# Moving the low-order subtraction of the first token block from GpSimd to VectorE

## The chip, the cores and the metric

The kernel runs on one core of one Trainium2 chip. The metric is device time in microseconds (us). Engines are named as the profile names them: PE (TensorE matmul) and PEld (its weight load), DVE (VectorE), ACT (ScalarE), POOL (GpSimd) and SP (SyncE, which here only issues DMAs).

## The reference

Three layers follow one another: windowed attention, a gated feed-forward layer on all tokens, and a layer of 8 experts of which each token uses one. The change lies in the second:

```python
def _moe_ref(x, w_gate, w_val, w_out, rms_g):        # x: 2304 x 512, d_ff = 1536
    rms = np.sqrt(np.mean(x * x, axis=-1, keepdims=True) + 1e-06)
    xn = x / rms * rms_g
    g = xn @ w_gate
    silu = g * (1.0 / (1.0 + np.exp(-g)))
    val = xn @ w_val
    return (silu * val @ w_out).astype(np.float32)
```

## The kernel before

**Split products.** Every matrix product is made of three matmuls. An operand is split into a high part, which is the operand rounded to the type fp32r, and a low part, which is the operand less its high part; the product is high x high + high x low + low x high (`split_mm`). So each operand costs one cast, always on ACT, and one subtraction, on DVE or POOL.

**Tokens, blocks, units.** The 2304 tokens are six parts of 384 (`subs`), gathered into four blocks (`BLOCKS`): the first two blocks hold two parts each, the last two hold one. The hidden width of 1536 is cut into 12 slices of 128. A *unit* is one slice for one part, so the first block has 24 units. For unit u the kernel does the following.

- `gate_val(u)`: 24 matmuls on PE write the gate product to one PSUM bank and the value product to another. In the first block these are nearly always the same two banks.
- `silu(u)`: ACT takes tanh of the gate bank into the tile `t` (L592), DVE makes silu times value in two steps (L593 reads the gate bank, L594 the value bank), ACT casts `t` to the high part `hh` (L595), and a subtraction writes the low part `hl` (L596). There is one tile `t`, and there are two each of `hh` and `hl`.
- `out_b(u - 1)`: 9 matmuls on PE with `hh` and `hl` of the unit before.

PE's order is `gate_val(u)`, `out_b(u - 1)`, `gate_val(u + 1)`. The last of these needs the two banks of unit u back, so it waits for L593 and L594 of unit u.

**Other work in the first block.** The weights of this layer come as 64-bit floating-point numbers and are converted on DVE while the first block runs: four instructions for each half slice, L400, L405, L408 and L415 (`w_conv`), with a square on ACT between (L425). The weights are then split (`w_split`): casts on ACT (L549), subtractions on DVE for gate and value (`wla`, L551) and on POOL for the output weights (`wlo`, L551). Also in between lie the normalisations of later parts: L333, L343, L345, L353, L355, L362 and L367 on DVE, L328, L351 and L364 on ACT, and one matmul with a matrix of ones on PE. The order on every engine is written out by the program (`manual_schedule`): after `silu(u)` a loop takes pieces of this other work up to a budget. The wait for an earlier result is taken in that order; an engine does not pass a waiting instruction.

From the second block on, L596 already runs on DVE.

Of the kernel before, what the change touches and what calls it, by code (L numbers as in the profile page):

```python
# [8 lines left out]
F32 = mybir.dt.float32  # L9
# [4 lines left out]
ALU = mybir.AluOpType  # L14
# [35 lines left out]
def attention_moe_moe_kernel(ctx, tc, qT, kT, vw, w1p, rms_g, wg2, wg2T, w2p, out):  # L50
    nc = tc.nc
# [243 lines left out]
    blocks, subs = [], []  # L295
# [275 lines left out]
    def gv_banks(u):  # L571
        n = subs[units[u][1]][2]
        if u == 1 and LEAD > 1:

            return bank[6:8]
        if u % 2 and len(blocks[n][2]) == 1:
            return bank[2:4] if n == len(blocks) - 1 else bank[6:8]
        return bank[0:2]
# [6 lines left out]
    def silu(u):  # L585
        k, i = units[u]
        nt = subs[i][1]
        g, v = (b[:, :nt] for b in gv_banks(u))
        t = t_p.tile([P, SUB], F32, name="t")[:, :nt]
        hh = hh_t["b", u] = h_p.tile([P, 512], F32R, name="hh")  # L590
        hl = hl_t["b", u] = h_p.tile([P, 512], F32R, name="hl")
        nc.scalar.activation(t, g, AF.Tanh, scale=0.5)  # L592
        nc.vector.scalar_tensor_tensor(out=t, in0=t, scalar=1.0, in1=g, op0=ALU.add, op1=ALU.mult)  # L593
        nc.vector.scalar_tensor_tensor(out=t, in0=t, scalar=0.5, in1=v, op0=ALU.mult, op1=ALU.mult)  # L594
        nc.scalar.copy(hh[:, :nt], t)  # L595
        (nc.gpsimd if subs[i][2] == 0 else nc.vector).tensor_tensor(  # L596
            out=hl[:, :nt], in0=t, in1=hh[:, :nt].bitcast(F32), op=ALU.subtract)

    def last_mm(w, h, banks, f0, f1):

# [231 lines left out]
    for u, (k, i) in enumerate(units):  # L832
# [4 lines left out]
        if u == 0:  # L837
            beside([norm1, conv], 3.0)
        silu(u)
        budget = BUDGET[n] + min(spare, 0.5)  # L840

# [213 lines left out]
    with tc.If(n_over > 0):  # L1055
        with tc.For_i(0, n_over, 1) as i:
            ex = nc.values_load(slot[0:1, bass.ds(i, 1)], engines=(ET.SP,), min_val=0, max_val=E - 1)
            row = nc.values_load(slot[0:1, bass.ds(i + NS, 1)], engines=(ET.SP,), min_val=0, max_val=E * NT - 2 * P)
            with tc.tile_pool(name="ovr", bufs=1) as o_p:
# [7 lines left out]
                for j in range(2):  # L1067
                    nc.gpsimd.indirect_dma_start(
                        out=xg[:, j], out_offset=None, in_=x2dram[:, :],
# [9 lines left out]
                for j in range(2):  # L1079
                    for f in range(NF2):  # L1080
# [4 lines left out]
                        out=out[:, :], out_offset=bass.IndirectOffsetOnAxis(ap=ix[:, j, 0:1], axis=0),  # L1085
# [48 lines left out]
```

## Time and profile before

| what | value |
|---|---|
| median of 3 runs | 909.71 us (909.12 to 910.42) |
| the profiled execution | 913.41 us |
| its span, first to last instruction | 911.5 us |
| PE busy over the span | 851.7 us (93%) |
| DVE busy | 671.6 us (74%) |
| ACT busy | 415.7 us (46%) |
| POOL busy | 252.7 us (28%) |

The profiled execution is one run of its own, 3.70 us above the median. Shares over the whole span mix stages: the first block, where L596 is on POOL, starts its first `silu` at 137.7 us, and its last L596 starts at 299.0 us.

### The profile page before, as it was taken

What the parts mean: (1) busy time and instruction counts of PE and PEld (TensorE: products, weight loads), DVE (VectorE), ACT (ScalarE), POOL (GpSimd) and SP (SyncE); (2) the same over time, 40 slices, a digit from 0 to 9 for tenths busy, and PEclk for the clock granted to TensorE, in tenths of its full rate; (3) what the DMA queues carried; (4) which work ended last, traced back from release to release, by engine and by line L of the source; (5) the groups of instructions that cost most, each with busy time, mean ns of one, the idle gap of its engine ahead of it and who ended that gap; (6) DMA issues with size and microseconds to landing.
All of it is one profiled execution on the core that took longest, in us unless ns stands there. A gap on an engine that the chain in (4) does not pass through costs nothing.

```text
span 911.5 us, 13574 instructions
## 1 busy us (share of the span) xinstructions
PE 851.7 (93%) x4667; PEld 778.3 (85%) x4667; DVE 671.6 (74%) x1535; ACT 415.7 (46%) x951; POOL 252.7 (28%) x268
## 2 busy tenths in 40 slices
PE   7999979998999999999999899999899999889994
PEld 7999968887889899999998789888678899778883
DVE  7789979999897677786589975986584665675462
ACT  5777864343343434322343333334463554564352
POOL 3357662332233000000312243232310330333021
PEclk9999998999999999999999999999899999999998
DMA  7888433333422620000100005323574664672010
GB/s 210 287 277 279 152 127 118 105 109 104 139 70 93 156 37 17 1 1 0 36 36 1 1 1 214 126 90 82 167 230 128 210 214 128 213 227 70 3 44 17
DMA packets 40895, 102.96 MB, mean 113 GB/s; under 512 B 10575, under 2 KB 15055, under 8 KB 40658
## 3 DMA queue, kind: packets, MB, share of 16 engines
q1 hardware_dynamic: 35090, 88.29, 30.8%
q0 software_dynamic: 5696, 13.14, 4.6%
q8 instruction: 78, 1.28, 0.6%
q14 instruction: 31, 0.25, 0.1%
HBM read 87.08 MB, written 19.57 MB: 117 GB/s over the span
## 4 chain that ended last, share of the span: by engine, by line
PE 48%; DVE 28%; issue 9%; DMA 6%; POOL 4%; ACT 3%; SPq 0%; DVEq 0%; POOLq 0%; ACTq 0%
PE bank L56 46%; DVE junk L658 6%; DMA out_dram<-x,ix 3%; DVE wla L551 3%; DVE wraw L405 2%; DVE wraw L408 2%; DVE t L594 2%; DVE wraw L415 2%; DVE t L593 2%; DVE wraw L400 2%; DMA sq<-x2dram,ix 1%; PE bank L222 1%; PE bank L785 1%; DVE xt L367 1%; ACT hh L595 1%
## 5 line engine op out<-in xcount | busy, mean ns | idle before, releaser
L56 PE MATMUL bank<-xt,wha 128*128 128x384 f32 (+3 forms) x1728 | 425.2, 331 | 23.0 <-DVE t L593 9.0
L56 PEld LDWEIGHTS bank<-xt,wha 128*128 128x128 f32 x1728 | 307.6, 191 | 42.2 <-DVE t L593 13.4
L56 PE MATMUL bank<-xt,wla 128*128 128x384 f32 (+3 forms) x864 | 284.7, 330 | 8.9 <-DVE wla L551 6.5
L56 PEld LDWEIGHTS bank<-xt,wla 128*128 128x128 f32 x864 | 165.1, 191 | 13.5 <-DVE wla L551 10.1
L56 PE MATMUL bank<-wlo,hh 128*128 128x512 f32 x384 | 152.8, 398 | 0.5 <-POOL wlo L551 0.5
L56 PE MATMUL bank<-who,hl 128*128 128x512 f32 x384 | 152.6, 397 | 0.4 <-DVE hl L944 0.4
L56 PE MATMUL bank<-who,hh 128*128 128x512 f32 x384 | 151.9, 395 | 0.1
L595 ACT CAST hh<-t 128x384 fp32r<-128x384 f32 x72 | 37.0, 513 | 206.4 <-DVE t L594 206.4
L944 DVE SCALAR_TENSOR_TENSOR hl<-bank,hh 128x512 fp32r<-128x512 f32 (+1 forms) x72 | 45.3, 629 | 86.7 <-ACT hh L943 86.6
L551 DVE TENSOR_TENSOR wla<-wraw,wha 128x512 fp32r<-128x512 f32 (+1 forms) x112 | 98.3, 877 | 5.1 <-ACT wha L549 4.6
L658 DVE SCALAR_TENSOR_TENSOR junk<-x,wg_bc 128x512 f32<-128x512 f32 x120 | 91.3, 812 | 0.0
L56 PEld LDWEIGHTS bank<-who,hl 128*128 128x128 f32 x384 | 72.8, 190 | 17.4 <-DVE hl L944 1.2
L549 ACT CAST wha<-wraw 128x512 fp32r<-128x512 f32 (+1 forms) x113 | 87.1, 771 | 0.0
L943 ACT ACTIVATE hh<-bank 128x512 fp32r<-128x512 f32 (+1 forms) x72 | 39.6, 550 | 104.0 <-PE bank L56 104.0
L56 PEld LDWEIGHTS bank<-wlo,hh 128*128 128x128 f32 x384 | 73.0, 190 | 11.9 <-POOL wlo L551 0.8
L56 PEld LDWEIGHTS bank<-who,hh 128*128 128x128 f32 x384 | 73.2, 191 | 11.4 <-issue 0.5
L56 PE MATMUL bank<-kt,qz 128*128 128x128 f32 x288 | 76.2, 406 | 5.5 <-DMA kt<-in_kT_dram 4.7
L551 POOL TENSOR_TENSOR wlo<-wraw,who 128x512 fp32r<-128x512 f32 x30 | 49.0, 1635 | 114.7 <-ACT who L549 114.6
L56 PEld LDWEIGHTS bank<-kt,qz 128*128 128x128 f32 x288 | 72.3, 334 | 6.1 <-DVE qz L165 4.7
L549 ACT CAST who<-wraw 128x512 fp32r<-128x512 f32 x111 | 68.8, 620 | 17.3 <-PE bank L56 17.0
L208 ACT ACTIVATE wraw<-sm,nm 128x128 f32<-128x128 f32 x144 | 56.2, 391 | 26.1 <-DVE nm L204 25.5
L551 DVE TENSOR_TENSOR wlo<-wraw,who 128x512 fp32r<-128x512 f32 x81 | 57.1, 705 | 8.6 <-ACT who L549 3.6
(153 smaller groups left out, 1009.5 us busy)
## 6 DMA issues: line engine op xcount, KB each, us to landing
wraw<-in_w2p_dram SPq DMA_DIRECT2D x64, 512.0 KB, 4.5
st<-in_w1p_dram SPq DMA_DIRECT2D x24, 768.0 KB, 4.4
wraw<-in_vw_dram SPq DMA_DIRECT2D x16, 512.0 KB, 5.1
qz<-in_qT_dram SPq DMA_DIRECT2D x32, 144.0 KB, 5.4
xdram<-wraw SPq DMA_DIRECT2D x16, 288.0 KB, 2.8
x2dram<-x SPq DMA_DIRECT2D x18, 256.0 KB, 2.4
kt<-in_kT_dram SPq DMA_DIRECT2D x15, 288.0 KB, 5.6
xr<-xdram SPq DMA_DIRECT2D x4, 768.0 KB, 5.5
```

Of the source, the lines that this page charges most:

```text
L56: nc.tensor.matmul(o, l, r, start=start, stop=stop)
L208: nc.scalar.activation(p[:, j], sm[:, j], AF.Exp, bias=nm[:, j:j + 1], scale=-1.0, accum_out=rs[:, j:j + 1])
L400: nc.vector.tensor_scalar(out=w, in0=hi, scalar1=3, scalar2=0x3FFFFFFF, op0=ALU.logical_shift_left, op1=ALU.bitwise_and)
L405: nc.vector.scalar_tensor_tensor(out=w, in0=lo, scalar=29, in1=w, op0=ALU.logical_shift_right, op1=ALU.bitwise_or)
L408: nc.vector.scalar_tensor_tensor(out=w, in0=hi, scalar=-0x40000000, in1=w, op0=ALU.bitwise_and, op1=ALU.bitwise_or)
L415: nc.vector.scalar_tensor_tensor(out=wf, in0=gt, scalar=TINY64 * TINY64, in1=wf, op0=ALU.is_ge, op1=ALU.mult)
L549: nc.scalar.copy(wh, src[:, r])
L551: e.tensor_tensor(out=wl, in0=src[:, r], in1=wh.bitcast(F32), op=ALU.subtract)))
L595: nc.scalar.copy(hh[:, :nt], t)
L658: nc.vector.scalar_tensor_tensor(out=junk, in0=x2, scalar=1.0, in1=wg_bc[:, e], op0=ALU.mult, op1=ALU.mult, accum_out=lg[:, j, e:e + 1])
L943: nc.scalar.activation(hh[:, :n], bank[k % 2][:, :n], AF.Relu, scale=1.0)
L944: nc.vector.scalar_tensor_tensor(out=hl[:, :n], in0=bank[k % 2][:, :n], scalar=0.0, in1=hh[:, :n].bitcast(F32), op0=ALU.max, op1=ALU.subtract)
```

## The change

For parts of the first block, L596 is issued on DVE instead of POOL. The place in the program is the same; the operands are the same.

```diff
         nc.vector.scalar_tensor_tensor(out=t, in0=t, scalar=1.0, in1=g, op0=ALU.add, op1=ALU.mult)
         nc.vector.scalar_tensor_tensor(out=t, in0=t, scalar=0.5, in1=v, op0=ALU.mult, op1=ALU.mult)
         nc.scalar.copy(hh[:, :nt], t)
-        (nc.gpsimd if subs[i][2] == 0 else nc.vector).tensor_tensor(
-            out=hl[:, :nt], in0=t, in1=hh[:, :nt].bitcast(F32), op=ALU.subtract)
+        nc.vector.tensor_tensor(out=hl[:, :nt], in0=t, in1=hh[:, :nt].bitcast(F32), op=ALU.subtract)
```

On DVE the 24 subtractions come in directly behind L594 of their units. Two neighbouring units in the middle of the first block show the two patterns; `wraw_109` is a converted weight slice, `st` the raw 64-bit words. The first of the two has a conversion's first step behind it:

```order
 L593 SCALAR_TENSOR_TENSOR t<-t,bank_65 128x384
 L594 SCALAR_TENSOR_TENSOR t<-t,bank_66 128x384
+L596 TENSOR_TENSOR hl<-t,hh 128x384
 L400 TENSOR_SCALAR wraw_109<-st 128x768
 L405 SCALAR_TENSOR_TENSOR wraw_109<-st,wraw_109 128x768
```

L400 now stands behind a subtraction that needs `hh` of the same unit from ACT. The next unit has a conversion's last step behind it:

```order
 L593 SCALAR_TENSOR_TENSOR t<-t,bank_65 128x384
 L594 SCALAR_TENSOR_TENSOR t<-t,bank_66 128x384
+L596 TENSOR_TENSOR hl<-t,hh 128x384
 L415 SCALAR_TENSOR_TENSOR wraw_109<-gt,wraw_109 128x768
 L400 TENSOR_SCALAR wraw_109<-st 128x768
```

Here L415 and the L400 of the next half slice have moved behind the subtraction. On POOL, before, the same part of the program reads (`wlo` and `who` are low and high parts of output weights):

```order
L596 TENSOR_TENSOR hl<-t,hh 128x384 x2
L551 TENSOR_TENSOR wlo_1556<-wraw_108,who_1555 128x512
L596 TENSOR_TENSOR hl<-t,hh 128x384 x2
L551 TENSOR_TENSOR wlo_1560<-wraw_108,who_1559 128x512
L596 TENSOR_TENSOR hl<-t,hh 128x384 x2
L551 TENSOR_TENSOR wlo_1558<-wraw_109,who_1557 128x512
```

and in the changed kernel:

```order
L551 TENSOR_TENSOR wlo_1558<-wraw_107,who_1557 128x512
L551 TENSOR_TENSOR wlo_1556<-wraw_108,who_1555 128x512
L551 TENSOR_TENSOR wlo_1560<-wraw_108,who_1559 128x512
L551 TENSOR_TENSOR wlo_1558<-wraw_109,who_1557 128x512
L551 TENSOR_TENSOR wlo_1556<-wraw_109,who_1555 128x512
```

Only the weight subtractions are left there in this stage. The orders of PE, ACT and SP hold the same instructions as before in the same sequence.

## Rows read from the trace of the kernel before

**Rows 1.** Chain of waits, 139 to 279 us, its shares by engine and line.
```profile
by line: DVE wraw L405 15.9%; DVE wraw L408 14.7%; DVE wraw L415 12.7%; DVE wraw L400 10.9%; PE bank L56 10.1%; DVE t L594 6.4%; DVE t L593 5.8%; DVE wla L551 4.9%; DVE xt L367 3.9%; issue 3.2%; DVE sq L333 2.2%; ACT sq L328 1.3%; DVE sq L3
```

**Rows 2.** Stages: us, PE, PEld, DVE, ACT, POOL busy (instructions), PE clock, DMA, GB/s.
```profile
139.00:279.00 140.00, 131.28 (x655) 118.91 (x653) 132.02 (x156) 55.98 (x95) 42.70 (x30) 0.97 0.32 103
224.00:231.00 7.00, 7.00 (x31) 6.73 (x30) 6.23 (x9) 2.63 (x5) 1.66 (x2) 0.76 0.39 134
279.00:305.00 26.00, 25.38 (x134) 23.72 (x134) 15.12 (x26) 11.02 (x23) 6.23 (x7) 1.00 0.36 135
305.00:455.00 150.00, 149.65 (x793) 139.60 (x793) 108.22 (x253) 49.20 (x90) 9.82 (x19) 1.00 0.12 27
```

**Rows 3.** Timeline of DVE, two units: start, duration, line, out<-in [idle before].
```profile
195.07 0.55 DVE L594 SCALAR_TENSOR_TENSOR t<-t,bank 128x384 f32<-128x384 f32 x1
...
197.12 1.66 DVE L408 SCALAR_TENSOR_TENSOR wraw<-st,wraw 128x768 int32<-128x768 int32 x1
...
200.49 0.56 DVE L594 SCALAR_TENSOR_TENSOR t<-t,bank 128x384 f32<-128x384 f32 x1
200.96 0.95 DVE L415 SCALAR_TENSOR_TENSOR wraw<-gt,wraw 128x768 f32<-128x768 f32 x1
201.83 1.39 DVE L400 TENSOR_SCALAR wraw<-st 128x768 int32<-128x768 int32 x1
203.25 1.93 DVE L405 SCALAR_TENSOR_TENSOR wraw<-st,wraw 128x768 int32<-128x768 int32 x1
...
208.67 0.55 DVE L594 SCALAR_TENSOR_TENSOR t<-t,bank 128x384 f32<-128x384 f32 x1
```

**Rows 4.** Timeline of POOL, the same two units.
```profile
196.31 1.66 POOL L596 TENSOR_TENSOR hl<-t,hh 128x384 fp32r<-128x384 f32 x1 [5.55 <-ACT hh L595]
201.73 1.06 POOL L596 TENSOR_TENSOR hl<-t,hh 128x384 fp32r<-128x384 f32 x1 [3.76 <-ACT hh L595]
202.76 1.60 POOL L551 TENSOR_TENSOR wlo<-wraw,who 128x512 fp32r<-128x512 f32 x1
```

**Rows 5.** Conversion lines over the whole run: shortest/median/longest ns, first and last start.
```profile
L400 DVE TENSOR_SCALAR wraw<-st x24: 531/555/1654, 36.7 to 274.2; 128x768 int32<-128x768 int32 x24
L405 DVE SCALAR_TENSOR_TENSOR wraw<-st,wraw x24: 920/960/1933, 37.3 to 275.8; 128x768 int32<-128x768 int32 x24
L408 DVE SCALAR_TENSOR_TENSOR wraw<-st,wraw x24: 926/958/1661, 41.6 to 276.8; 128x768 int32<-128x768 int32 x24
```

**Rows 6.** Timeline of DVE in the second block's first unit, where L596 is on DVE.
```profile
304.75 0.56 DVE L594 SCALAR_TENSOR_TENSOR t<-t,bank 128x384 f32<-128x384 f32 x1
305.89 0.56 DVE L596 TENSOR_TENSOR hl<-t,hh 128x384 fp32r<-128x384 f32 x1 [0.58 <-ACT hh L595]
306.36 0.68 DVE L628 COPY x<-bank 128x512 f32<-128x512 f32 x1
```

**Rows 7.** Timeline of DVE, its four longest idle stretches from 139 to 279 us.
```profile
168.22 0.56 DVE L343 TENSOR_SCALAR sq<-bank 128x384 f32<-128x384 f32 x1 [1.00 <-PE bank L56]
...
229.73 0.56 DVE L594 SCALAR_TENSOR_TENSOR t<-t,bank 128x384 f32<-128x384 f32 x1 [0.70 <-PE bank L56]
...
232.60 1.23 DVE L367 TENSOR_TENSOR xt<-xr,xt 128x384 fp32r<-128x384 f32 x1 [1.32 <-ACT xt L364]
...
272.81 0.56 DVE L343 TENSOR_SCALAR sq<-bank 128x384 f32<-128x384 f32 x1 [1.17 <-PE bank L56]
```

**Rows 8.** Timeline of DVE: L400 with POOL's weight subtraction beside it.
```profile
274.15 1.65 DVE L400 TENSOR_SCALAR wraw<-st 128x768 int32<-128x768 int32 x1
```

**Rows 9.** Timeline of DVE: two L362 at the first block's end.
```profile
292.05 1.78 DVE L362 SCALAR_TENSOR_TENSOR xr<-xr,gs_sb,sq 128x384 f32<-128x384 f32 x2
```

**Rows 10.** Timeline of PE: two waits for DVE.
```profile
223.68 0.62 PE L56 MATMUL bank<-xt,wha 128*128 128x384 f32 x2 [2.05 <-DVE t L593]
...
311.59 0.59 PE L56 MATMUL bank<-sq,ones 128*128 128x384 f32 x1 [0.35 <-DVE t L594]
```

**Rows 11.** Groups of POOL by line, 139 to 305 us: busy us, mean ns, idle before.
```profile
L596 POOL TENSOR_TENSOR hl<-t,hh 128x384 fp32r<-128x384 f32 x24 | 31.2, 1300 | 115.2 <-ACT hh L595 115.2
```

## Prediction

> **What bounds the kernel now.** I read the stages first, then the chain of waits in the stage of the change, then the timelines of the engines that the chain names.
>
> The change touches units of the first block, from 139 to 300 us. Up to 279 us PE is busy for 131.28 of 140 us and DVE for 132.02, so either could set the pace; from 279 to 455 us PE stands still for less than 1 us [rows 2]. The chain decides: from 139 to 279 us PE holds 10.1% of it, and the rest lies almost wholly on DVE, the four conversion lines alone with over 50% [rows 1]. PE's idle 8.7 us in this stage are mostly waits for L593, one of 2.05 us among them [rows 10]. So up to 279 us a microsecond of DVE time is a microsecond of the kernel, as far as DVE does not stand idle anyway. Behind that PE is full, and a delay of PE's start at 279 us is carried to the end.
>
> The timelines then show that a subtraction on POOL isn't free for DVE. At 196.31 POOL starts L596, and DVE's L408 at 197.12 lasts 1.66 us. In the next unit POOL has L596 from 201.73, and DVE's L400 at 201.83 lasts 1.39 us; the weight subtraction from 202.76 lies beside an L405 of 1.93 us [rows 3, 4]. The same lines have medians of 0.958, 0.555 and 0.960 us [rows 5]. Each POOL subtraction thus already costs DVE a stall.
>
> **What the change adds to DVE.** In the second block, where DVE has this work, L594 starts at 304.75, L596 at 305.89 after 0.58 us of idle time for the cast on ACT, and the next instruction at 306.36: 1.61 us from L594 to what follows L596 [rows 6]. Without L596 the next instruction starts 0.47 us after L594 (200.49 to 200.96) [rows 3]. So a unit gains 1.61 - 0.47 = 1.14 us on DVE, more than half of it waiting. The wait has no cover: what could fill it (L400, L415) stands behind L596, and DVE takes its instructions in order. ACT cannot be earlier, since the cast needs L594; nor does it get later, since its own order is unchanged. 20 of the 24 units lie ahead of 279 us: 20 x 1.14 = **+22.8 us**.
>
> **What it gives back.** L408 gets 1.66 - 0.96 = 0.70 us back, L400 gets 1.39 - 0.56 = 0.83 us [rows 3, 5]. I went through the 20 units on DVE's timeline: nine are like the first pattern (0.70), eight like the second or near it (0.83), and three have no stretched instruction, because DVE was idle or read from PSUM while POOL worked. 9 x 0.70 + 8 x 0.83 = **-12.9 us**.
>
> **What the weight subtractions on POOL do then.** They stay, and they still stall DVE. Before, they followed a subtraction on POOL, and L405 lost 1.93 - 0.96 = 0.97 us [rows 3]. Now they start at about the time of the instruction behind L596; where that was so before, the L400 behind it took 1.65 us, a loss of 1.10 [rows 8]. Seven units have this pattern: between 0 and 7 x 0.13 = 0.9 us. No row says which instruction gets there first, so I take the middle: **+0.5 us**.
>
> **What is absorbed.** Where DVE waited for something that doesn't come later by the new work, the 1.14 us fill the wait. There are four such stretches of any size ahead of 279 us: 1.00, 0.70, 1.32 and 1.17 us [rows 7]. Filled are 1.00, then 0.44 (that unit's net growth, 1.14 - 0.70, is less than its wait), 1.1 and 1.1: **-3.7 us**, rounded. The bounds: nothing is absorbed, or all of DVE's idle time there, 140 - 132.02 = 8.0 us [rows 2]; most of the rest are gaps of 0.1 us ahead of L594, which stay, hence the value near the lower end.
>
> Sum at 279 us: 22.8 - 12.9 + 0.5 - 3.7 = +6.7 us.
>
> **Behind 279 us.** DVE is busy for only 15.12 of 26 us, and PE is full [rows 2], so most of the last four units' 1.14 us hide behind PE. One does not: the last normalisation of the block is a chain over DVE, a load and ACT to the second block's first L593, and PE waited 0.35 us for what follows it [rows 10], so that chain has no slack. Its unit pays 1.14 and gets back the stretch of two L362, which took 1.78 us [rows 9] where two instructions of this operation and shape take some 1.1 (0.56 each, as L594) [rows 6]: +1.14 - 0.65 = **+0.5 us**. The rest of the program has the same order and starts that much later.
>
> Total: **+7.2 us**. The profiled execution of before took 913.41 us (span 911.5, the rest around it); the sum makes 920.6 there. Against the median, 909.71 us, it makes **916.9 us**, on the assumption that what lies around the span stays the same.
>
> **The rivals.**
>
> *Faster: POOL's hold is longer than the stretched rows show.* If POOL kept DVE out for the whole of each L596, 31.2 us over the 24 units [rows 11], removing them would give 31.2 against 24 x 1.14 = 27.4 us added: -3.8 us, 905.9 us. It decides from 1.14 us of returned time a unit. For it: wherever POOL's L596 meets a DVE instruction on SBUF, that one is stretched. Against it: the rows give back 0.70 and 0.83, since part of POOL's recorded time passes while it waits itself (1.66 us behind a running L405, 1.06 otherwise) [rows 3, 4]. Chance 0.06.
>
> The Trainium skill has this rule: "SBUF — State Buffer", section "SBUF: two separate sides", says that VectorE and GpSimd share one port pair by an exclusive lock, that an instruction with two SBUF inputs takes it against a GpSimd instruction that reads SBUF, and that the loser blocks for the whole instruction. By it, read on POOL's recorded durations, the kernel would get faster, as this rival; by the stretched rows it gets 7.2 us slower. The trace agrees that one waits for the other, and it shows that the recorded duration is not the hold.
>
> *No change.* DVE's idle time is 8.0 us ahead of 279 us and 26 - 15.12 = 10.9 us behind it [rows 2], more than the net +9.9 (22.8 - 12.9). If it could all be used, PE would be fed as before: 909.7 us. Against it: the larger part lies behind 279 us, and by then PE has waited. Chance 0.06.
>
> *Slower by more, through PE's clock.* After its wait of 2.05 us [rows 10] PE's granted clock had a mean of 0.76 over the next 7 us [rows 2], that is, some 3.4 us at the lower level, 1.2 GHz, and (1 - 0.76) x 7 = 1.7 us of matmul time lost. PE's waits grow now, to about 1.8 us in each of some seven pairs of units. One such stretch a pair is nearly hidden, since DVE is the later engine; if two came in a row, a pair would lose 1.7 us more: 7 x 1.7 = 11.9, so 928.8 us. Against it: a second stretch directly behind the first is not seen in this stage. Chance 0.08.
>
> **How the numbers follow.** The forecast, +7.2 us, has a chance of 0.80 and a range of its own from the bounds: with all idle time absorbed and none of the small terms, 22.8 - 12.9 - 8.0 = +1.9 (911.6); with nothing absorbed and the small terms full, 9.9 + 0.9 + 0.5 = +11.3 (921.0). About 0.2% or 1.8 us is what a measurement of this kernel can tell from no change. I give 911.8 to 921.5 as the range; the three rivals, 0.20 together, lie outside. Slower: 0.80 + 0.08 = 0.88; same 0.06; faster 0.06.
>
> **What would show it.** In the changed kernel, L596 on DVE ahead of 300 us with some 0.58 us of idle time before each (14 us over 24); L408 at 0.96 us in the first pattern's units, where it had 1.66; stretched instructions only beside the weight subtractions; a pair of units that lasted 208.67 - 195.07 = 13.6 us [rows 3] lasting 13.6 + 2 x 1.14 - 0.70 - 0.83 = 14.4 us; the first L593 of the second block some 7 us later, and the stages behind it as long as before. Wrong would be the prediction if DVE's instructions stayed stretched where POOL has nothing to do (then slower), if PE showed long stretches at the lower clock (slower), or if DVE's idle time ahead of 279 us had shrunk by much more than 4 us (nearer to no change).

## The result and the profile after

The changed kernel takes 916.28 us (median of 5 runs, 911.08 to 920.01) against 909.12 us before (median of 5, 907.3 to 910.42): ratio 1.0068, 95% interval 1.004 to 1.0097. It is slower, by 6.2 us by the ratio and 7.2 us by the medians; the forecast was +7.2. A second set of runs of the same kernel gave 915.91 us against 908.32, ratio 1.0085 (1.0055 to 1.0114).

The two profiled executions say the opposite at first sight: the span after is 909.2 us, before it was 911.5. So the first thing to read is where in the span the change shows. The stages after, with the columns of [rows 2] (the second row is a stretch in which PE's clock fell):

```profile
139.00:279.00 140.00, 125.06 (x617) 113.55 (x616) 124.42 (x168) 54.53 (x93) 17.00 (x9) 0.96 0.32 102
271.00:278.00 7.00, 6.10 (x26) 6.06 (x26) 5.98 (x10) 2.78 (x4) 0.00 (x0) 0.76 0.00 1
279.00:305.00 26.00, 26.00 (x137) 24.12 (x136) 20.15 (x33) 8.85 (x18) 3.45 (x4) 1.00 0.20 81
305.00:455.00 150.00, 149.37 (x790) 138.79 (x789) 106.71 (x251) 49.81 (x92) 9.85 (x19) 1.00 0.15 32
```

From 139 to 279 us the profile records 617 matmuls on PE where it recorded 655, and DVE was busy for less time, not more: 124.42 us against 132.02. A stalled instruction counts as busy, a wait for ACT as idle; busy time alone would have hidden the loss. POOL's busy time fell from 42.70 to 17.00 us.

The chain of waits of that stage, by line, now has the cast on ACT in it:

```profile
by line: DVE wraw L405 12.5%; DVE wraw L408 11.7%; DVE wraw L415 11.4%; DVE wraw L400 10.6%; PE bank L56 9.4%; DVE t L594 6.9%; DVE hl L596 6.4%; ACT hh L595 6.3%; DVE t L593 5.8%; DVE wla L551 5.7%; DVE xt L367 2.9%; issue 2.6%; DVE sq L33
```

L596 holds 6.4% of it and L595 6.3%; neither is among the shares shown for the kernel before [rows 1]. DVE's timeline for the two units of [rows 3]:

```profile
197.85 0.55 DVE L594 SCALAR_TENSOR_TENSOR t<-t,bank 128x384 f32<-128x384 f32 x1
198.99 0.56 DVE L596 TENSOR_TENSOR hl<-t,hh 128x384 fp32r<-128x384 f32 x1 [0.58 <-ACT hh L595]
199.47 0.55 DVE L400 TENSOR_SCALAR wraw<-st 128x768 int32<-128x768 int32 x1
...
201.04 0.96 DVE L408 SCALAR_TENSOR_TENSOR wraw<-st,wraw 128x768 int32<-128x768 int32 x1
...
204.84 0.56 DVE L596 TENSOR_TENSOR hl<-t,hh 128x384 fp32r<-128x384 f32 x1 [0.58 <-ACT hh L595]
205.31 0.95 DVE L415 SCALAR_TENSOR_TENSOR wraw<-gt,wraw 128x768 f32<-128x768 f32 x1
206.18 1.65 DVE L400 TENSOR_SCALAR wraw<-st 128x768 int32<-128x768 int32 x1
207.87 0.96 DVE L405 SCALAR_TENSOR_TENSOR wraw<-st,wraw 128x768 int32<-128x768 int32 x1
...
212.32 0.55 DVE L594 SCALAR_TENSOR_TENSOR t<-t,bank 128x384 f32<-128x384 f32 x1
```

From L594 to what follows L596 are 199.47 - 197.85 = 1.62 us. L408 is back at 0.96. Only the weight subtraction still stalls DVE: L400 lasts 1.65, and L405 no longer pays. On POOL it is the only instruction in this time:

```profile
205.40 2.01 POOL L551 TENSOR_TENSOR wlo<-wraw,who 128x512 fp32r<-128x512 f32 x1 [12.45 <-DVE hl L596]
```

The pair takes 212.32 - 197.85 = 14.47 us, where it took 13.60.

To compare kernels I use landmarks on DVE's timeline: the first L593 of the program (unit 0), the L593 of unit 20, the first L593 of the second block (unit 24), and the first subtraction of the expert stage (L944 before, L943 after). All are start times in us.

| execution | unit 0 | unit 20 | unit 24 | expert stage | from there to the span's end | span |
|---|---|---|---|---|---|---|
| before | 138.23 | 279.04 | 304.10 | 616.87 | 294.6 | 911.5 |
| before, second profile | 139.64 | 279.82 | 304.81 | 617.56 | 288.8 | 906.4 |
| changed | 138.10 | 285.81 | 311.63 | 624.35 | 284.9 | 909.2 |
| changed, second profile | 138.26 | 285.94 | 311.76 | 624.48 | 287.6 | 912.1 |

Unit 24 comes 6.8 to 7.7 us later in each comparison, and the expert stage begins 6.8 to 7.6 us later. Only behind that do the executions differ without order: the expert stage took 284.9 to 294.6 us. The first profile of before had the longest one, and that alone makes its span longer than that of the changed kernel. From unit 24 to the expert stage all four executions of the table take 312.7 to 312.8 us.

### The profile page after: what moved, and what is told of

Same layout as the page of the kernel before. It is cut to its first block, busy times and chain, and to the rows that moved or that the text cites. A ratio compares the mean times of both kernels' runs of the same rounds, so it can differ in the third digit from the quotient of the medians.

```text
span 909.2 us, 13562 instructions
## 1 busy us (share of the span) xinstructions
PE 848.6 (93%) x4667; PEld 776.5 (85%) x4667; DVE 672.3 (74%) x1559; ACT 415.8 (46%) x951; POOL 225.7 (25%) x244
## 4 chain that ended last, share of the span: by engine, by line
PE 51%; DVE 28%; issue 8%; DMA 5%; POOL 4%; ACT 4%; SPq 0%; DVEq 0%; POOLq 0%; ACTq 0%
PE bank L56 48%; DVE junk L657 6%; DVE wla L551 3%; DMA out_dram<-x,ix 3%; DVE t L594 2%; DVE hl L596 2%; ACT hh L595 2%; DVE wraw L405 2%; DVE wraw L415 2%; DVE wraw L408 2%; DVE t L593 2%; DVE wraw L400 2%; PE bank L784 1%; PE bank L222 1%; DVE xt L367 1%
## 5 line engine op out<-in xcount | busy, mean ns | idle before, releaser
L56 PE MATMUL bank<-xt,wha 128*128 128x384 f32 (+3 forms) x1728 | 424.2, 330 | 25.9 <-DVE t L593 14.4
L595 ACT CAST hh<-t 128x384 fp32r<-128x384 f32 x72 | 36.9, 513 | 207.5 <-DVE t L594 205.2
L551 POOL TENSOR_TENSOR wlo<-wraw,who 128x512 fp32r<-128x512 f32 x30 | 51.1, 1703 | 251.8 <-DVE hl L596 134.1
L943 DVE SCALAR_TENSOR_TENSOR hl<-bank,hh 128x512 fp32r<-128x512 f32 (+1 forms) x72 | 45.3, 629 | 78.9 <-ACT hh L942 72.9
L596 DVE TENSOR_TENSOR hl<-t,hh 128x384 fp32r<-128x384 f32 x72 | 40.2, 559 | 41.7 <-ACT hh L595 40.0
```

Of the source, the lines that this page charges most:

```text
L56: nc.tensor.matmul(o, l, r, start=start, stop=stop)
L551: e.tensor_tensor(out=wl, in0=src[:, r], in1=wh.bitcast(F32), op=ALU.subtract)))
L596: nc.vector.tensor_tensor(out=hl[:, :nt], in0=t, in1=hh[:, :nt].bitcast(F32), op=ALU.subtract)
L943: nc.vector.scalar_tensor_tensor(out=hl[:, :n], in0=bank[k % 2][:, :n], scalar=0.0, in1=hh[:, :n].bitcast(F32), op0=ALU.max, op1=ALU.subtract)
```

## The experiments

My theory: L596 on DVE costs 1.14 us a unit, of which more than half is the wait for the cast, and gives back the stall that POOL's L596 had caused; DVE sets the pace up to unit 20, so the net of both shows. The rivals: the wait lies in time that DVE has to spare; or POOL's hold is worth more, or nothing.

### The subtraction deferred by one piece of other work

```diff
-        nc.vector.tensor_tensor(out=hl[:, :nt], in0=t, in1=hh[:, :nt].bitcast(F32), op=ALU.subtract)
+        def low():
+            nc.vector.tensor_tensor(out=hl[:, :nt], in0=t, in1=hh[:, :nt].bitcast(F32), op=ALU.subtract)
+
+        if subs[i][2] > 0:
+            low()
+            return None
+        return low
...
-    def beside(tasks, budget):
+    def beside(tasks, budget, then=None):
...
             cost = can[0].piece()
             budget -= cost
+            if then and cost > 0:
+                then()
+                then = None
...
```

Expected: 

> The changed kernel, with L596 of the first block issued one piece of other work later on VectorE, so that the wait for the cast on ScalarE is covered; nothing else moves. My theory (half of the 1.14 us a unit is waiting, and it is on the path): a unit gains only 0.47 us on VectorE, 20 units gain 9.5 us, 12.9 us are given back, so the second block's first L593 starts 1 to 3 us earlier than before (304.1 us there), and the kernel takes 906.5 to 909 us. Rival (the wait falls into time in which VectorE has nothing urgent, and the 0.56 us of work are what costs): as the changed kernel, some 916 us and 311 us.

Measured: 904.98 us against 907.19, ratio 0.9976 (0.9955 to 0.9996), a gain of 2.2 us; I had set the expected times against 909. Unit 24 starts at 300.67 us, 3.4 us earlier than before and 11.0 us earlier than in the changed kernel. DVE's timeline (L599 is what was L594, L603 the subtraction, L420, L405 and L410 the conversion's lines):

```profile
199.03 0.56 DVE L599 SCALAR_TENSOR_TENSOR t<-t,bank 128x384 f32<-128x384 f32 x1
199.50 0.95 DVE L420 SCALAR_TENSOR_TENSOR wraw<-gt,wraw 128x768 f32<-128x768 f32 x1
200.37 0.55 DVE L603 TENSOR_TENSOR hl<-t,hh 128x384 fp32r<-128x384 f32 x1
200.84 1.66 DVE L405 TENSOR_SCALAR wraw<-st 128x768 int32<-128x768 int32 x1
202.53 0.96 DVE L410 SCALAR_TENSOR_TENSOR wraw<-st,wraw 128x768 int32<-128x768 int32 x1
```

The subtraction starts without idle time; over the block's 24 units the idle time ahead of it is 2.1 us, of which 0.6 us are a wait for the cast. That wait is in one unit, where the subtraction still follows L599 directly; in 21 units one instruction lies between, in two units two. The same work on the same engine, mostly one instruction later, turns the loss into a small gain. The rival on spare time is out; at 300.67 us the gain is a little larger than the 1 to 3 us expected.

### The subtraction without its wait

```diff
+        was = hh_t["b", u - 1] if u > 0 and subs[i][2] == 0 else hh
-        nc.vector.tensor_tensor(out=hl[:, :nt], in0=t, in1=hh[:, :nt].bitcast(F32), op=ALU.subtract)
+        nc.vector.tensor_tensor(out=hl[:, :nt], in0=t, in1=was[:, :nt].bitcast(F32), op=ALU.subtract)
```

Expected: 

> The changed kernel, but in the first block L596 subtracts the high part of the unit before, which is long there (so the low parts are other numbers): the same instruction at the same place without its wait. My theory: as the deferred one, 0.47 us a unit, 906.5 to 909 us, with the second block's first L593 at 301 to 303 us. Rival (the work costs, not the wait): 916 us.

Measured: 903.57 us, ratio 0.9958 (0.9938 to 0.9978); unit 24 at 301.09 us. On DVE's timeline L597, the subtraction, starts 0.59 us after L594 where the changed kernel has 198.99 - 197.85 = 1.14:

```profile
199.91 0.55 DVE L594 SCALAR_TENSOR_TENSOR t<-t,bank 128x384 f32<-128x384 f32 x1
200.50 0.56 DVE L597 TENSOR_TENSOR hl<-t,hh 128x384 fp32r<-128x384 f32 x1
200.97 0.95 DVE L415 SCALAR_TENSOR_TENSOR wraw<-gt,wraw 128x768 f32<-128x768 f32 x1
```

By its median it gains 3.6 us, a little more than expected; its landmark is where the theory put it, within 0.5 us of that of the deferred kernel. Two ways of taking the wait away agree. Here the place of the instruction is that of the changed kernel, so it is the wait and not the place that costs.

### The wait alone

```diff
         (nc.gpsimd if subs[i][2] == 0 else nc.vector).tensor_tensor(
             out=hl[:, :nt], in0=t, in1=hh[:, :nt].bitcast(F32), op=ALU.subtract)
+        if subs[i][2] == 0:
+            nc.vector.tensor_copy(look, hh[:, 0:1].bitcast(F32))
```

Expected: 

> The kernel before, L596 of the first block on GpSimd, and behind L594 a copy of one element a row from the high part on VectorE: the wait for ScalarE alone, with next to no work. My theory: 1.14 us to the copy's start and some 0.1 us for it, less 0.47, is 0.75 us a unit, 15 us over 20 units, less 3 to 4 us that fall into idle time; nothing is given back: +11 to +12 us, 920 to 921 us. Rival (waiting costs nothing since VectorE has slack): 909 to 911 us.

Measured: 921.16 us, ratio 1.0157 (1.0122 to 1.0191), that is, +14 us; unit 24 at 317.76 us. DVE's timeline shows the copy, and a stall besides:

```profile
201.07 0.55 DVE L594 SCALAR_TENSOR_TENSOR t<-t,bank 128x384 f32<-128x384 f32 x1
202.21 0.15 DVE L599 COPY look<-hh 128x1 f32<-128x1 f32 x1 [0.58 <-ACT hh L595]
202.28 0.55 DVE L400 TENSOR_SCALAR wraw<-st 128x768 int32<-128x768 int32 x1
202.86 1.65 DVE L405 SCALAR_TENSOR_TENSOR wraw<-st,wraw 128x768 int32<-128x768 int32 x1
```

L400 starts 1.21 us after L594 instead of 0.47: 0.74 us a unit for a wait with a one-element copy behind it, 20 x 0.74 = 14.8 us. Against the 907.19 of its own comparison the loss is 2 us more than the 11 to 12 expected, though its interval, 11.1 to 17.3 us, holds the 12. Counted from unit 0 (138.92), unit 20 (292.05) lies 12.3 us later than in the first profile of before, so that idle time absorbed some 2.5 us, not 3 to 4; at the start of the expert stage (631.11) it is 13.6 us. With POOL's work kept, the wait is the dearest variant of all: DVE waits for ACT and is then stalled by POOL as before.

### No subtraction at all

```diff
-        nc.vector.tensor_tensor(out=hl[:, :nt], in0=t, in1=hh[:, :nt].bitcast(F32), op=ALU.subtract)
+        if subs[i][2] == 0:
+            hl_t["b", u] = zero
+        else:
+            nc.vector.tensor_tensor(out=hl[:, :nt], in0=t, in1=hh[:, :nt].bitcast(F32), op=ALU.subtract)
...
```

The low part of the first block is a tile of zeros (`zero`), so this kernel leaves out the low-order term there.

Expected: 

> The changed kernel without L596 in the first block: the low part there is a constant tile of zeros, so the low-order term is left out and the matmuls stay. It shows what GpSimd's hold costs before, by itself. My theory (0.70 to 0.83 us of VectorE time a unit, 12.9 us in all, of which TensorE's 8.7 us of idle time allow the larger part to show): 5 to 8 us faster than before, 901 to 904 us. Rival (the stretched instructions are hidden): the time of before, 909 us.

Measured: 895.93 us against 907.19, ratio 0.9875 (0.9848 to 0.9903): 11.3 us faster, where I expected at most 8. Unit 20 starts at 265.71 us, 13.3 us earlier than before. The stage from 139 to 279 us, with the columns of [rows 2]:

```profile
139.00:279.00 140.00, 138.45 (x721) 127.77 (x720) 124.73 (x170) 60.81 (x104) 15.11 (x13) 1.00 0.36 117
```

and its chain of waits by line (L594 and L595 are what were L593 and L594):

```profile
by line: PE bank L56 62.3%; DVE wraw L405 6.9%; DVE wraw L415 5.7%; DVE wraw L408 5.5%; DVE t L595 2.8%; DVE wraw L400 2.8%; DVE t L594 2.7%; DVE wla L551 2.4%; DVE xt L367 2.1%; issue 1.6%; DVE xr L362 1.1%; DVE sq L333 1.1%; ACT xt L364 0
```

PE is now the bound, with 62.3% of the chain. My upper limit had counted only PE's idle time before, 8.7 us. It left out that PE's busy time shrinks as well. From unit 0 to unit 24 this kernel takes 152.16 us, 13.7 and 13.0 us less than the two profiles of before. PE's idle time in that stretch fell by 7.8 and 8.7 us. The granted clock was 0.50, the lower level, for 8.4 and 5.1 us of it before and for 1.3 us here; half of the difference, 3.6 and 1.9 us, is matmul time won. The remaining 2.3 to 2.4 us are not accounted for. The zeros are not what the clock needs: the deferred kernel, with its true low parts, has a mean of 0.99 from 139 to 279 us. So POOL's 24 subtractions alone, which look free in a profile of POOL, cost the kernel before some 11 us. The rival, that the stretched instructions are hidden, is out.

### The weight subtractions on DVE as well

In the deferred kernel, the first block's `wlo` go to DVE too, at the end of their units' other work (their cost in the budget is kept at zero, so that nothing else moves):

```diff
-            eng = {"a": nc.gpsimd if k < 2 else nc.vector, "o": nc.vector if n == 1 else nc.gpsimd}
+            eng = {"a": nc.gpsimd if k < 2 else nc.vector, "o": nc.vector if n <= 1 else nc.gpsimd}
...
```

Expected: 

> The deferred kernel, with the first block's weight subtractions (wlo) on VectorE too, at the end of their units' other work, so that GpSimd does nothing beside VectorE in that block. My theory (each wlo on GpSimd costs VectorE 1.0 to 1.1 us of waiting, and 0.61 us when VectorE does it): ten or eleven times 0.4 to 0.5 us, 4 to 5 us earlier than the deferred kernel at the second block's first L593 (300.7 us there), so some 296 us, and 900 to 902 us in all. Rival (after the deferral TensorE is the bound and nothing more is to be had): 300 us and 905 us. The kernel without L596 reached 290.3 us, so TensorE's bound lies at or below that.

Measured: 903.22 us against 908.32, ratio 0.9948 (0.9929 to 0.9967); unit 24 at 297.96 us. This execution began unit 0 at 138.89 us, 0.8 us later than the deferred kernel's (138.12); from unit 0 to unit 24 it takes 159.07 us against 162.55, a gain of 3.5 us where 4 to 5 were expected. No conversion line is stretched any more on DVE's timeline:

```profile
199.53 0.55 DVE L603 TENSOR_TENSOR hl<-t,hh 128x384 fp32r<-128x384 f32 x1
199.99 0.55 DVE L405 TENSOR_SCALAR wraw<-st 128x768 int32<-128x768 int32 x1
...
203.51 0.95 DVE L420 SCALAR_TENSOR_TENSOR wraw<-gt,wraw 128x768 f32<-128x768 f32 x1
204.38 0.68 DVE L556 TENSOR_TENSOR wlo<-wraw,who 128x512 fp32r<-128x512 f32 x1
204.98 0.54 DVE L598 SCALAR_TENSOR_TENSOR t<-t,bank 128x384 f32<-128x384 f32 x1
```

L405 lasts 0.55 us where the deferred kernel has 1.66, for 204.98 - 204.38 = 0.60 us of work. The time lies above the 900 to 902 us expected, too. What is missing against the expectation is not settled by a run; the chain of this kernel has 19.7% on PE, where the deferred one has 7.7%, so a part of it fits PE having become the limit of more units. This is the best of the complete kernels by its median, and faster than both given ones.

### The weight subtractions alone

The same edit on the kernel before, with L596 left on POOL.

Expected: 

> The kernel before with only the weight subtractions (wlo) of the first block on VectorE and L596 left on GpSimd: which of GpSimd's two jobs there is worth moving when neither waits. My theory: as in the pair above, 0.4 us won per wlo, 4 us in all, second block's first L593 at 300 us, 903 to 905 us. Rival (the two subtractions on GpSimd, back to back, hold VectorE no longer than the one): no change, 304 us and 907 us.

Measured: 904.25 us against 908.32, ratio 0.9955 (0.9937 to 0.9974); unit 24 at 301.41 us, with unit 0 at 139.42. From the one to the other are 161.99 us, 3.9 less than the 165.87 of the first profile of before and 3.2 less than the 165.17 of the second: about as the theory has it. Each of POOL's two jobs is worth moving as long as nothing waits. Both together (159.07 us) gain 2.9 to 3.5 us more than either alone by this landmark; by their medians in one comparison, 903.22 and 904.25 us, the intervals overlap.

### Both given kernels again

Expected: 

> The changed kernel once more, for a second profile. My theory: the first block's cost is the same each time (second block's first L593 at 311 to 312 us), and the spread of 9 us over its runs comes from the last stage, from some 680 us on. Rival (the spread comes from the first block, by the clock): the L593 moves by several us.

Expected: 

> The kernel before once more, for a second profile. My theory: the second block's first L593 again at 304 us, the first hidden-layer subtraction of the last stage again at 617 us, and a last stage several us shorter than the 294 us of the first profile. Rival: as the first profile, 911 us of span.

Measured: 915.91 us for the changed kernel, 908.27 us in the one run of the kernel before, and the landmarks of the table above. In the changed kernel all landmarks agree within 0.16 us. In the kernel before the second profile starts the block 1.4 us later and lies 0.7 us later at unit 24 (304.81, not 304.1), and its expert stage took 288.8 us, 5.8 us less. So most of the difference between two executions of one kernel lies here in the expert stage, as expected; two profiles of each do not show that for the whole spread of the runs. What in the stage varies was not tried.

## Why the prediction was right

**The bound.** DVE's chain up to unit 20, a full PE behind it: a delay of 6.77 us at unit 20 (first profiles) was 7.53 at unit 24 and 7.48 at the expert stage, so it is carried through. Forecast were +6.7 at 279 us and +7.2 in all.

**The terms,** read from the changed kernel's timeline:

- *Added:* 1.61 us expected from L594 to what follows L596; 1.60 to 1.62 measured. The wait is 0.58 us in each of the 24 units, 13.9 us.
- *Given back:* 12.9 us expected, some 13.8 found, instruction by instruction. L408 and L400 gave back 0.70 and 0.83 as listed. I had taken the unit at 271 us as one of three that give nothing; there the weight subtraction moved into DVE's idle time, and an L400 of 1.65 us [rows 8] became 0.55.
- *The weight subtractions:* I took the middle between 0 and 0.9. It was near the upper end: L400 lasts 1.65 or 1.66 us in six units; in the seventh L405 lasts 1.93, as long as the L415 that was stretched there before. So 0.8 us.
- *Absorbed:* 3.7 us expected, some 2.5 found. Three of the four idle stretches of [rows 7] filled as said (1.00 and 1.32 vanished, 0.70 became 0.24). The fourth did not: 1.17 became 1.03, and another of 0.27 came ahead of it.
- *Behind 279 us:* 0.5 us expected, 0.76 found from unit 20 to unit 24 in the first profiles and 0.83 in the second. Of the 0.76, 0.54 lie in the chain that was named (the two L362 took 1.15 us instead of 1.78), and 0.22 in the units ahead of it, which I had taken to be hidden.

The idle stretch that stayed shows the rival of PE's clock in small. PE's wait for L593, on PE's timeline of the changed kernel, was 2.14 us there:

```profile
271.90 0.62 PE L56 MATMUL bank<-xt,wha 128*128 128x384 f32 x2 [2.14 <-DVE t L593]
```

and the mean granted clock over the 7 us from 271 us was 0.76 (row above), as after the wait of 2.05 us before [rows 10]. PE came later by about what DVE came later, and the idle stretch stayed. It did not spread to each pair of units, as the rival had it: after 140 us the changed kernel has three stretches at the lower level up to unit 24, where the first profile of before has two, and the pair shown above took 14.47 us, 14.4 were expected.

A wait of this size was not always followed by a lower clock, as the prediction's rival supposed. In the second profile of the kernel before, PE waited as long at the same place:

```profile
225.09 0.61 PE L56 MATMUL bank<-xt,wha 128*128 128x384 f32 x2 [2.07 <-DVE t L593]
```

and the 7 us that follow, with the columns of [rows 2], have a mean of 1.00, where the first profile had 0.76:

```profile
225.00:232.00 7.00, 6.91 (x37) 6.52 (x38) 6.72 (x10) 2.83 (x5) 1.85 (x2) 1.00 0.41 135
```

What else decides is open.

The three deviations up to unit 20, -0.9, +0.3 and +1.2 us, largely cancel: the corrected sum there is +7.3, and counted from unit 0 the first profile of the changed kernel (147.71 us) is 6.9 and 7.5 us longer than the two of before (140.81 and 140.18). So no step failed; the sizes of four terms were off by 0.3 to 1.2 us, in part in opposite directions. That the forecast meets the difference of the medians to a tenth is luck: the interval of the measurement runs from 3.6 to 8.8 us.

**The rival "faster",** that POOL holds DVE for its whole recorded time, is out by the deferred kernel: it adds 0.47 us a unit, and with 1.3 us given back (31.2 / 24) it would have reached PE's limit, where the kernel without L596 has unit 24 at 290.3 us. It stands at 300.7. The Trainium skill's "Perfetto Trace Analysis", section "Optimizing Scalar/DVE Operations", says that moving work between GpSimd and VectorE might not help, since they share a read port. These runs show both outcomes: the move lost 7.2 us with the wait and gained 2.2 without it. A POOL subtraction costs DVE 0.70 to 0.83 us of stall, the same subtraction on DVE costs 0.47 us, or 1.14 with its wait.

## What to carry to other kernels

Work on one engine can cost another its time without any wait between them: compare the longest duration of a form with its median, and look at what ran beside it. When an instruction moves to an engine that takes its work in order, its input's latency moves along; place it behind one instruction that is ready, and the price falls to its own duration (here from 1.14 to 0.47 us, from a loss of 7 us to a gain of 2). And compare two kernels by landmarks of the stage that was changed: here the spans of two single profiles had the wrong sign.

## What was not expected of the hardware

The 24 subtractions on POOL cost the kernel before 11.3 us (ratio 0.9875), more than PE's idle time in the stage, 8.7 us. A part of it is PE's clock, whose mean there was 0.97 and 0.98 in the two profiles before and 1.00 without them. A wait of 2.05 us was followed by a stretch at the lower clock in one execution of the kernel before, and a wait of 2.07 us at the same place in another was not. The expert stage of one and the same program took 284.9 and 287.6 us, or 294.6 and 288.8 us, in two executions each. And a copy of one element a row, with the wait that it brings, cost 14 us when placed 24 times on the engine that sets the pace.
